# Another scheme of 20 products, with the first tap of a convolution moved to ScalarE and the sums of y to GpSimd

## Chip, cores, metric

One core of one Trainium2 chip. The metric is device time in microseconds of the whole program. Before: 2664.77 us, median of 3 runs (2663.69 to 2666.85).

## The reference, cut to what matters

```python
# x: (8, 4096, 192); 7-tap causal convolution, one softmaxed filter per head (8 heads of 24 channels)
out = np.einsum('hk,bskhg->bshg', w, x_unf)        # 32768 tokens of 192
h = x @ w_in                                       # 192 -> 2048
g = h * np.clip(h + 3.0, 0.0, 6.0) / 6.0
return g @ w_out                                   # 2048 -> 192
```

## The kernel before

Tokens are done in 32 blocks of 1024; the first is done directly, the other 31 in two stages each. In the **h stage**, 88 half matmuls with a fast scheme give h; ScalarE makes the relu and VectorE the gate, and g stays in SBUF as eight "places" (0 to 7), each 128 x 4 x 512 (four "units"). While it runs, GpSimd already makes some sums of places, unit by unit (`EARLY`), into extra places (8 and up). In the **product stage**, g @ w_out is made of 20 products of such places (or sums of them) with prepared sums of weights, two products side by side in one step, ten steps. VectorE makes large sums of places, GpSimd's queue issues DMA copies that add (`'sum', 'dma'`). A node is a partial result in one half of a PSUM bank. A copy (ScalarE) takes a node out of PSUM, a seed (ScalarE) puts such a copy into a node's half bank so that products are added to it, and a join (VectorE) adds a node and a copy. The convolution of the next block (seven taps on VectorE), the swap of y's halves by DMA and four sums of y run beside it. Each engine takes its instructions in the order of the program.

```python
EARLY = [(8, 3, 7, '+'), (3, 2, 3, '+'), (9, 2, 8, '+'), (10, 1, 0, '+'), (10, 10, 8, '-')]
STEPS = [
    ('conv',), ('mm', (6, 9, 56, 0, 1), (0, 0, 7, 1, 1)), ('conv',),
    ('mm', (4, 6, 56, 0, 0), (2, 3, 7, 1, 0)), ('sum', 6, 6, 9, '+'),
    ('mm', (9, 13, 49, 0, 1), (5, 8, 32, 1, 1)), ('sum', 2, 5, 6, '-'), ('copy', 7, (0, 0)),
    # ... cut: six more steps
    ('mm', (0, 1, 4, 0, 0), (1, 19, 2, 1, 0)),  # ... cut: joins and three outputs
]
# 'mm': two of (place, form of weights, node, half of a PSUM bank, opens the node)
# 'sum', to, a, b, sign: VectorE adds two places; 'sum', 'dma', to, from: a DMA adds
# 'copy', node, half tile | 'seed', node, ... | 'join', node, to, from, other, sign
# 'conv': next tap of the next block | 'ysums': the four sums of y

def tap(part, k, t):
    c = c_sb[:, k : k + 1]
    to = y[:, part, t : t + W]
    if k == 0:
        nc.vector.tensor_scalar(out=to, in0=x[:, part, t : t + W], scalar1=c, scalar2=None, op0=ALU.mult)
    else:
        nc.vector.scalar_tensor_tensor(out=to, in0=x[:, part, k + t : k + t + W], scalar=c, in1=to,
                                       op0=ALU.mult, op1=ALU.add)

def open(self, node, k):     # a node takes one half of a bank; two nodes can share a bank
    b = next((b for b, u in self.used.items() if k not in u), None)
    if b is None:
        b = take()
    # ... cut
```

## Time and profile before

| | before |
|---|---|
| median, us | 2664.77 |
| busy share of TensorE, VectorE, ScalarE, GpSimd | 92%, 82%, 49%, 43% |
| mean granted TensorE clock | 0.984 |
| product stage, h stage (means of the 30 blocks that another follows), us | 44.8, 38.0 |

The means by stage in this document are worked out from the trace's timeline of TensorE: from the first matmul with product weights to the first with h weights, and on to the next block.

### The profile page before, as it was taken

What the parts mean: (1) busy time and instruction counts of PE and PEld (TensorE: products, weight loads), DVE (VectorE), ACT (ScalarE), POOL (GpSimd) and SP (SyncE); (2) the same over time, 40 slices, a digit from 0 to 9 for tenths busy, and PEclk for the clock granted to TensorE, in tenths of its full rate; (3) what the DMA queues carried; (4) which work ended last, traced back from release to release, by engine and by line L of the source; (5) the groups of instructions that cost most, each with busy time, mean ns of one, the idle gap of its engine ahead of it and who ended that gap; (6) DMA issues with size and microseconds to landing.
All of it is one profiled execution on the core that took longest, in us unless ns stands there. A gap on an engine that the chain in (4) does not pass through costs nothing.

```text
span 2669.4 us, 40470 instructions
## 1 busy us (share of the span) xinstructions
PE 2458.6 (92%) x15976; PEld 981.8 (37%) x15976; DVE 2194.1 (82%) x2558; ACT 1312.1 (49%) x2233; POOL 1158.3 (43%) x856
## 2 busy tenths in 40 slices
PE   9988999999999999999899889999999998899888
PEld 5433343333333333433333333343333433333333
DVE  8688887888888888888888788888888878888786
ACT  7344555445554454544455444555445554455544
POOL 2634543445433455333553335543345433454334
PEclk9999999999999999999999999999999999999999
DMA  5143324433244432344323443324433244332443
GB/s 131 37 84 64 57 47 83 84 67 64 42 78 84 79 64 39 69 84 83 60 49 59 84 83 60 53 55 83 84 65 63 41 83 83 66 63 39 84 72 60
DMA packets 277934, 182.20 MB, mean 68 GB/s; under 512 B 208432, under 2 KB 213552, under 8 KB 277744
## 3 DMA queue, kind: packets, MB, share of 16 engines
q0 software_dynamic: 50688, 97.79, 21.8%
q1 hardware_dynamic: 226904, 81.69, 15.6%
q8 instruction: 125, 2.05, 0.3%
q14 instruction: 65, 0.53, 0.1%
q10 hardware_dynamic: 152, 0.13, 0.0%
HBM read 31.72 MB, written 25.17 MB: 21 GB/s over the span
## 4 chain that ended last, share of the span: by engine, by line
PE 64%; DVE 20%; issue 7%; DMA 5%; ACT 3%; SPq 0%; DVEq 0%; ACTq 0%
PE psum L338 46%; PE psum L621 16%; DVE g L568 5%; DMA y<-y 5%; DVE y L294 3%; DVE extra L568 3%; DVE parts L574 3%; DVE y L315 2%; DVE y L290 2%; PE psum L465 2%; DVE g L348 1%; ACT parts L639 1%; ACT r L344 1%; ACT psum L645 1%; SPq L307 0%
## 5 line engine op out<-in xcount | busy, mean ns | idle before, releaser
L621 PE MATMUL psum<-g,w_t 128*32 128x512 f32 x7440 | 1156.3, 607 | 119.1 <-ACT psum L645 66.4
L338 PE MATMUL psum<-y,w_in 64*128 64x512 f32 x3664 | 884.5, 591 | 0.0
L568 POOL TENSOR_TENSOR extra<-g 128x512 f32<-128x512 f32 x248 | 361.8, 1459 | 970.0 <-DVE g L348 970.0
L344 ACT ACTIVATE r<-psum,half 128x512 f32<-128x512 f32 x1024 | 642.0, 689 | 242.2 <-PE psum L338 232.5
L621 PE MATMUL psum<-extra,w_t 128*32 128x512 f32 x2480 | 578.3, 619 | 83.4 <-ACT psum L647 41.7
L348 DVE SCALAR_TENSOR_TENSOR g<-r,psum 128x512 f32<-128x512 f32 x1024 | 641.1, 680 | 5.4 <-ACT r L344 1.5
L338 PEld LDWEIGHTS psum<-y,w_in 64*128 64x128 f32 x3664 | 416.1, 187 | 397.4 <-issue 376.2
L621 PEld LDWEIGHTS psum<-g,w_t 128*32 128x32 f32 x7440 | 313.8, 112 | 623.3 <-issue 351.3
L338 PE MATMUL psum<-y,w_in_t 64*128 64x512 f32 x1984 | 523.5, 591 | 0.0
L639 ACT COPY parts<-psum 64x512 f32<-64x512 f32 x310 | 179.8, 580 | 692.8 <-PE psum L621 451.6
L430 DVE TENSOR_TENSOR psum<-psum,p 128x512 f32<-128x512 f32 x496 | 328.0, 696 | 224.2 <-PE psum L338 210.4
L294 DVE SCALAR_TENSOR_TENSOR y<-x,c_sb,y 128x1536 f32<-128x1536 f32 (+1 forms) x206 | 373.4, 1819 | 5.4
L338 PEld LDWEIGHTS psum<-y,w_in_t 64*128 64x128 f32 x1984 | 242.8, 186 | 200.9 <-issue 145.8
L621 PEld LDWEIGHTS psum<-extra,w_t 128*32 128x32 f32 x2480 | 143.6, 114 | 420.6 <-issue 263.0
L568 POOL TENSOR_TENSOR g<-g 128x512 f32<-128x512 f32 x124 | 158.1, 1275 | 289.6 <-DVE g L348 287.2
L574 DVE TENSOR_TENSOR parts<-parts 64x512 f32<-64x512 f32 x155 | 106.6, 688 | 156.3 <-ACT parts L639 152.2
L568 POOL TENSOR_TENSOR extra<-extra 128x512 f32<-128x512 f32 x124 | 218.4, 1762 | 9.7
L645 ACT COPY psum<-parts 64x512 f32<-64x512 f32 x279 | 163.2, 585 | 117.6 <-PE psum L621 110.8
L423 ACT COPY psum<-psum 128x512 f32<-128x512 f32 x248 | 138.9, 571 | 148.2 <-PE psum L338 133.5
L631 POOL DMA_DIRECT2D g<-g x124 | 152.2, 1950 | 86.0 <-DVE g L568 65.1
L568 DVE TENSOR_TENSOR g<-g 128x2048 f32<-128x2048 f32 x62 | 169.8, 2739 | 4.2
L568 POOL TENSOR_TENSOR extra<-g,extra 128x512 f32<-128x512 f32 x124 | 158.5, 1278 | 0.0
(60 smaller groups left out, 1019.5 us busy)
## 6 DMA issues: line engine op xcount, KB each, us to landing
g<-g POOLq DMA_DIRECT2D x124, 512.0 KB, 8.8
g<-extra POOLq DMA_DIRECT2D x62, 512.0 KB, 11.3
out_dram<-xt SPq DMA_DIRECT2D x384, 64.0 KB, 2.0
y<-y SPq DMA_DIRECT2D x62, 384.0 KB, 5.6
x<-in_x_dram SPq DMA_DIRECT2D x55, 388.5 KB, 5.6
stage<-in_moe_w_in_dram SPq DMA_DIRECT2D x16, 192.0 KB, 4.3
stage<-in_moe_w_out_dram SPq DMA_DIRECT2D x8, 384.0 KB, 5.0
x<-in_x_dram SPq DMA_DIRECT2D x7, 384.0 KB
```

What stands on the lines that cost most here:

```text
L294: nc.vector.scalar_tensor_tensor(out=to, in0=x[:, part, k + t : k + t + W], scalar=c, in1=to, op0=ALU.mult, op1=ALU.add,)
L338: nc.tensor.matmul(out=psum[:, b], lhsT=w[r], rhs=y[r, third_of_y], start=start, stop=stop, skip_group_check=onto,)
L344: nc.scalar.activation(r6, h, ACT.Relu, bias=half[:], scale=1.0 / 6.0)
L348: nc.vector.scalar_tensor_tensor(out=out, in0=r6, scalar=1.0, in1=h, op0=ALU.min, op1=ALU.mult)
L423: nc.scalar.copy(out=psum[:, bank["b"]], in_=psum[:, bank["a"]])
L430: nc.vector.tensor_tensor(out=psum[:, to], in0=psum[:, bank["b"]], in1=self.p5[:], op=ALU.add)
L568: engine.tensor_tensor(out=g_place(to)[:, u], in0=g_place(a)[:, u], in1=g_place(b)[:, u], op={"+": ALU.add, "-": ALU.subtract}[op],)
L574: nc.vector.tensor_tensor(out=out, in0=x, in1=y, op=op)
L621: nc.tensor.matmul(out=psum[col : col + QS, nodes.at[node][0]], lhsT=w[:, u, e * QS : (e + 1) * QS], rhs=g_place(place)[:, u], start=bool( ...
L631: nc.gpsimd.dma_start(out=g_place(args[1])[:, us], in_=g_place(args[2])[:, us], accum_op=ALU.add,)
L639: nc.scalar.copy(out=tile_half(*at), in_=nodes(node))
L645: nc.scalar.copy(out=nodes(node), in_=tile_half(*at))
```

## The change

Its intent: another scheme of 20 products, ordered anew, should make TensorE wait less for sums, seeds and joins; a fourth extra place makes room for sums that come earlier. VectorE gives its first tap to ScalarE and its sums of y to GpSimd. All else that the diff touches serves that: other sums of weights, a fifth tile for parts, two output buffers in place of four.

```diff
     EARLY = [
-        (8, 3, 7, '+'), (3, 2, 3, '+'), (9, 2, 8, '+'), (10, 1, 0, '+'), (10, 10, 8, '-'),
+        (8, 2, 3, '+'), (9, 1, 0, '-'), (9, 9, 3, '+'), ('dma', 3, 7), (10, 8, 7, '+'),
+        (11, 6, 10, '+'),
     ]
     STEPS = [
# (all steps replaced; the new ones:)
+        ('conv0',), ('conv',), ('mm', (4, 7, 56, 0, 1), (0, 0, 7, 1, 1)), ('conv',),
+        ('mm', (4, 6, 32, 0, 1), (2, 3, 7, 1, 0)), ('conv',),
+        ('mm', (5, 8, 32, 0, 0), (9, 4, 45, 1, 1)), ('conv',), ('copy', 7, (0, 0)),
+        ('seed', 49, 0, (0, 0), 1), ('seed', 54, 1, (0, 0), 1), ('sum', 'dma', 4, 6),
+        ('mm', (10, 13, 49, 0, 0), (11, 15, 48, 1, 1)), ('sum', 5, 5, 11, '+'),
+        ('copy', 45, (0, 0)), ('seed', 4, 0, (0, 0), 1), ('sum', 2, 5, 8, '-'),
+        ('seed', 41, 1, (0, 0), 1), ('mm', (0, 1, 4, 0, 0), (8, 5, 54, 1, 0)),
+        ('copy', 48, (0, 0)), ('sum', 6, 9, 2, '+'), ('seed', 1, 1, (0, 0), 1),
+        ('join', 49, (0, 1), None, (0, 0), 1), ('sum', 'dma', 9, 7),
+        ('mm', (6, 17, 42, 0, 1), (5, 18, 50, 1, 1)), ('conv',), ('seed', 9, 1, (0, 1), 1),
+        ('copy', 54, (0, 0)), ('conv',), ('mm', (4, 9, 56, 0, 0), (7, 10, 9, 1, 0)),
+        ('sum', 4, 4, 6, '-'), ('copy', 42, (1, 0)), ('seed', 18, 1, (1, 0), 1),
+        ('join', 50, (1, 1), None, (0, 0), 1), ('mm', (4, 14, 40, 0, 1), (2, 16, 18, 1, 0)),
+        ('sum', 5, 1, 5, '+'), ('ysums',), ('join', 32, (2, 0), None, (1, 1), -1),
# ... cut: two more steps, joins, three outputs; among them
+        ('out', 4, (16, 4)), ('copy', 41, (0, 0)), ('join', 32, (2, 0), (2, 0), (0, 0), -1),
+        ('join', 9, (1, 0), None, (0, 0), 1), ('two', 8, (2, 1), (1, 0), (1, 1), -1),
+        ('out', 2, (32, 8)), ('copy', 2, (0, 0)), ('join', 1, (0, 1), None, (1, 0), -1),
@@ the first tap
-            if k == 0:
+            if k == 0 and first is nc.scalar:
+                nc.scalar.mul(to, x[:, part, t : t + W], c)
+            elif k == 0:
@@ the sums of y
             elif op == "ysums" and more:
-                y_sums()
+                y_sums(nc.gpsimd)
@@ the places for sums
-        extra = ss.tile([P, 3, UNITS, N], F32, name="extra")
-        parts_ = cs.tile([P, 4, N], F32, name="parts")
+        extra = ss.tile([P, 4, UNITS, N], F32, name="extra")
+        parts_ = cs.tile([P, 5, N], F32, name="parts")
# ... cut: sums of weights, forms, output buffers, order at the start
```

## The prediction

> **What bounds the kernel now.** I read the page's busy shares first, then a table by stage, then what TensorE waits for, then the queues of VectorE and GpSimd at the start of one product stage. A block of 1024 tokens has two stages: the h stage (88 half matmuls and their gates) and the product stage (10 steps of two products each, steps 1 to 10 below). There are 31 such blocks. The table by stage, one block (span, then busy us and instructions of PE, PEld, DVE, ACT, POOL, then PE clock):
>
> ```profile
> 1211.90:1256.50 44.60, 38.26 (x322) 10.85 (x320) 37.98 (x30) 13.48 (x24) 18.08 (x12) 0.96 0.52 92
> 1256.50:1294.50 38.00, 38.00 (x180) 19.27 (x176) 30.65 (x51) 27.13 (x46) 17.68 (x15) 1.00 0.21 39
> ```
>
> The h stage is TensorE without a gap; its 38.0 us can't shrink by this change. The product stage takes 44.6 us, though one unhindered step is a row of 32 records in 3.64 us with its tail, 3.44 us when the next follows (64 records in 7.07): ten steps are 34.4 + 0.2 = 34.6 us. So 10.0 us a block are lost there, 310 us in all; that is the whole prize. Who causes it, from the waits of TensorE:
>
> ```profile
> PE psum L621 <- DVE parts L574: 94.2, 60, 3.4
> PE psum L621 <- ACT psum L645: 66.6, 63, 1.4
> PE psum L621 <- ACT psum L647: 41.7, 31, 1.3
> ```
>
> These make 202 us, 6.5 us a block; the rest is slow matmuls at half clock after the gaps, and ends of steps. The releasers are joins and seeds: VectorE and ScalarE come late. Why, the timeline at the stage's start shows, VectorE first, then GpSimd (start, us, what):
>
> ```profile
> 1213.94 1.81 DVE L290 TENSOR_SCALAR y<-x,c_sb 128x1536 f32<-128x1536 f32 x1
> 1215.78 2.62 DVE L294 SCALAR_TENSOR_TENSOR y<-x,c_sb,y 128x1536 f32<-128x1536 f32 x1
> 1218.33 3.37 DVE L568 TENSOR_TENSOR g<-g,extra 128x2048 f32<-128x2048 f32 x1
> 1221.80 3.19 DVE L568 TENSOR_TENSOR g<-g 128x2048 f32<-128x2048 f32 x1
> 1224.90 1.81 DVE L294 SCALAR_TENSOR_TENSOR y<-x,c_sb,y 128x1536 f32<-128x1536 f32 x1
> 1226.63 2.28 DVE L568 TENSOR_TENSOR extra<-g,extra 128x2048 f32<-128x2048 f32 x1
> ```
> ```profile
> 1215.50 1.29 POOL L568 TENSOR_TENSOR extra<-g,extra 128x512 f32<-128x512 f32 x1
> 1216.74 2.81 POOL L568 TENSOR_TENSOR extra<-g 128x512 f32<-128x512 f32 x1
> 1219.62 3.21 POOL L568 TENSOR_TENSOR extra<-extra 128x512 f32<-128x512 f32 x1
> ```
>
> The two engines take turns. A tap alone is 1.81 us, beside GpSimd 2.62; a sum alone 2.28, beside it 3.37 or 3.19; GpSimd's 1.29 becomes 2.81 and 3.21. The ends fit strict alternation: GpSimd ends at 1216.79, the tap at 1218.40, GpSimd at 1219.55, the sum at 1221.70, GpSimd at 1222.83, the next sum at 1224.99. Net holds: tap 1.66, GpSimd's sum 1.14, large sum 2.15. The one-source first tap (1.81) beside GpSimd is not slowed. So VectorE runs without a pause from the stage's start until step 5, which waits for it.
>
> **What the Trainium skill says.** (1) GPSIMD Engine Reference, section 1, Specifications: GpSimd shares its SBUF interfaces with VectorE and contends with VectorE instructions that have two SBUF inputs. The trace agrees: 1.81 against 2.62. (2) VectorE: DVE Perf Modes, the section on the TRN2 errata: a two-source fp32 addition takes (N+151)/0.96 ns; for N = 2048 that is 2291, the trace has 2.28 us. (3) TensorE: Matmul & The Clock Gate, Part 1: after an idle window of about 3.4 us the array falls to half clock, until about 3.4 us of work. Here it fell even in stages with shorter gaps (PE clock 0.96 above), so a longer gap will hardly escape.
>
> **The change part by part.** Times count from the start of a product stage; waits are those of the changed program as built, in its order on each engine. The number of products, matmuls, transposes and stores is the same.
>
> *First tap to ScalarE.* VectorE loses 1.81 us. On ScalarE a 128x128 scaling took 390 ns and a 128x512 one 721, so 0.86 ns an element; 1536 elements are estimated at 1.6 us. ScalarE's last relu ends at 1.35 (1213.28 - 1211.93), so the product is there at 2.95; VectorE, free at 2.1, starts its second tap then. Gain on the path 0.9 us, not 1.8.
>
> *Early sums and four taps in front.* The last unit's gate ends at 2.1. GpSimd then owes 5 sums and one DMA issue, VectorE four taps, all with two SBUF inputs, so they alternate: sum 8 until 3.4; then tap 1.66, sum 1.14, tap, sum (place 9 at 9.0), tap (10.6; the DMA issue of 1.2 beside it), sum (place 10 at 11.8), tap (13.4), sum: place 11 at 3.4 + 4 x 1.66 + 4 x 1.14 = 14.6. Step 3 needs 9 at about 9.5: no wait. Step 4 starts at 10.3 and needs the last quarter of 11 at 12.9: it waits 1.7 and ends at 15.6. Step 5 runs to 19.0.
>
> *The chain to step 6.* VectorE: 5 += 11 starts at 14.6 (it needs 11), 16.9; 2 = 5 - 8, 19.2; then 6 = 9 + 2, then the join of node 49, 0.7, which shares a bank with step 6's node, so step 6 waits for it. But 6 = 9 + 2 overwrites what the DMA sum 4 += 6 reads, and this DMA is queued on GpSimd behind sum 11: two issues from 14.6 to 17.0. A DMA sum of 512 KB landed after 5.2 us at the least and 10.2 in the middle; at the measured 187 GB/s each takes 2.8 us of transfer. The second lands between 21 and 23, say 22. So the sum ends at 24.3, the join at 25.0, step 6 starts at 25.1 where step 5 ended at 19.0: **6 us of gap**. Without the DMA it would be 22.3, still over 3 us.
>
> *Steps 6 to 10.* Step 6 to 28.5, 7 to 32.0. The sum 4 = 4 - 6 overwrites step 7's operand and feeds step 8: TensorE waits 2.3. Step 8 34.3 to 37.8; step 9, whose bank waits for a join, 38.0 to 41.4; a seed in the other half of step 9's bank takes 0.7; step 10 to 45.6. Sum of the waits: 1.7 + 6.0 + 2.3 + 0.2 + 0.7 = 10.9, with 34.6 of work 45.5. To this comes half clock after the 6 us gap: a window of 3.4 us costs 1.7 of work when it falls on running steps; I take 1.5. **Product stage: 47 us**, was 44.6.
>
> *Sums of y to GpSimd.* VectorE loses 2.62 us and the wait for the swap of y (0.87), which were in front of step 10's joins. That is what the change gains. The swap starts at about 28.6 (two taps after the join) and takes 6.8 as in the chain before (1242.86 to 1249.67); GpSimd's four sums of 1.27, some delayed by joins, end near 43, before the h stage needs them. Free, but what held step 10 is then no longer VectorE's total but the chain above. VectorE also gets 14 joins in place of 11 (3 x 0.69).
>
> *The end of the stage.* Only the last output is put off, so after step 10 ScalarE copies (0.6), VectorE does two joins (1.4), then ScalarE frees a bank, which the fifth matmul of the h stage needs: there at 2.8 after the start, where TensorE wants it at 1.7; with the two copies behind it the h stage loses about 1.4 us: 39.4.
>
> *Start.* One more weight sum and three more negations, about 2 us once, mostly beside matmuls.
>
> Sum: 47.0 + 39.4 = 86.4 against 82.6, 3.8 x 31 = 118, and 2: 2665 + 120 = **2785 us**.
>
> **The rivals.** A: *the relief wins*. VectorE loses 4.4 us a block and steps wait less: were the DMA sum to land by 19 and the clock to stay, the stage is 34.6 + 1.7 + 3.3 + 3.2 = 42.8 and the block 82.2 with the late h start, 81 without: 2615 to 2650. For it speaks that seeds and joins caused all waits before and that now most seeds come a step earlier; against it, that three whole sums in a row stand between place 11 and step 6. B: *the chain of sums as above but no clock loss and an early DMA (21)*: stage 44.6, block 84: 2710. C: *the DMA is slower*, 10 us or more as its median says, and half clock lasts two windows: stage 49 to 50, block 89: 2860. D: if GpSimd did not alternate with VectorE but came first, place 11 is there at about 10, the DMA lands at 18 and the stage is near 42: as A. The measured alternation speaks against it.
>
> **Range and chances.** Between B and C lies most of it: 2700 to 2850. Faster by 2% needs under 80.9 us a block, which even A barely reaches: 0.06. Within 2% is 80.9 to 84.3, A's worse half and B: 0.14. Slower: 0.80.
>
> **What would show it.** In the profile after: the largest wait of TensorE is on the join (same line, VectorE) before step 6, 5 to 7 us, 31 times; one on the sum of VectorE before step 8, 2.3 us; one on GpSimd's sum in step 4, 1 to 2 us; PE clock under 1.0 in most product stages; 39 to 40 us for the h stage; the swap's wait on VectorE gone; the first tap on ScalarE near 1.6 us. Wrong if the product stage is under 43 us: then the DMA sum lands earlier or the two engines do not take turns as I read it. If the h stage alone grows, my count of late joins was right and the chain wrong.

## The result, and the profile after

2864.07 us, median of 4 runs (2862.03 to 2867.15), beside 2665.23 us of before: ratio 1.0747, 95% interval 1.0728 to 1.0766. It is slower, as predicted, but by 199 us where 120 were predicted, and outside the range. (Ratios here are the mean time of one kernel's runs over that of the other's of the same rounds, so not quite the ratio of the medians quoted.)

The same table by stage for one block of the changed kernel (span, then busy us and instructions of PE, PEld, DVE, ACT, POOL, then PE clock, DMA share and GB/s):

```profile
1202.98:1251.80 48.82, 38.41 (x322) 12.25 (x320) 36.85 (x26) 10.25 (x17) 26.15 (x16) 0.93 0.39 71
1251.80:1291.30 39.50, 38.72 (x178) 19.45 (x176) 31.91 (x51) 27.86 (x48) 17.86 (x15) 1.00 0.31 55
```

The product stage grew from 44.6 to 48.8 us and the h stage from 38.0 to 39.5. The product stage has a clock of 0.93 where it had 0.96. Over the 30 blocks that another follows the means are 49.3 (was 44.8) and 39.5 (was 38.0). What TensorE waits for (us in total, times, longest):

```profile
PE psum L639 <- DVE parts L592: 201.4, 37, 8.2
PE psum L639 <- DVE g L581: 77.0, 31, 2.5
PE psum L345 <- DVE parts L592: 23.5, 30, 0.8
PE psum L639 <- POOL extra L581: 23.1, 30, 0.8
PE psum L639 <- ACT psum L659: 21.3, 31, 0.7
```

The waits for seeds of ScalarE, 108 us before, are down to 21; but one join now costs 201 us. The timeline of TensorE in that block shows where, with the idle time before a row in brackets:

```profile
1217.70 0.62 PE L639 MATMUL psum<-extra,w_t 128*32 128x512 f32 x2 [0.80 <-POOL extra L581]
...
1228.64 9.04 PE L639 MATMUL psum<-g,w_t 128*32 128x512 f32 x64 [6.45 <-DVE parts L592]
...
1240.16 4.05 PE L639 MATMUL psum<-g,w_t 128*32 128x512 f32 x34 [2.48 <-DVE g L581]
...
1248.14 3.74 PE L639 MATMUL psum<-g,w_t 128*32 128x512 f32 x32 [0.68 <-ACT psum L659]
```

Counted from the stage's start at 1202.98, these are step 4's wait for place 11 (at 14.7), the gap before step 6 (starts at 25.7), the wait before step 8 and that before step 10. Steps 6 and 7 are the row of 64 records: 9.04 us, where 64 records took 7.07 before. That is the half clock. VectorE and then GpSimd in the same stage:

```profile
1205.84 10.69 DVE L301 SCALAR_TENSOR_TENSOR y<-x,c_sb,y 128x1536 f32<-128x1536 f32 x4 [0.76 <-ACT y L295]
1217.68 4.62 DVE L581 TENSOR_TENSOR g<-g,extra 128x2048 f32<-128x2048 f32 x2 [1.16 <-POOL extra L581]
1225.57 2.29 DVE L581 TENSOR_TENSOR g<-extra,g 128x2048 f32<-128x2048 f32 x1 [3.27 <-DMA g<-g]
1227.90 0.68 DVE L592 TENSOR_TENSOR parts<-psum,parts 64x512 f32<-64x512 f32 x1
```
```profile
1214.98 2.67 POOL L581 TENSOR_TENSOR extra<-g,extra 128x512 f32<-128x512 f32 x1
1217.60 2.43 POOL L587 DMA_DIRECT2D g<-g  x2
```

GpSimd's first row is the sum to place 11. The four taps take 10.69 us where four alone take 7.2: they alternate with GpSimd. GpSimd's last sum ends at 1217.65, VectorE's two large sums start on it, then VectorE waits 3.27 us for the DMA that GpSimd could issue only then, makes 6 = 9 + 2, and the join lets TensorE go on.

The last block tells the same without taps, since no block follows whose convolution is to be made. VectorE, then TensorE, in the last product stage (it starts at 2803.63):

```profile
2814.23 4.62 DVE L581 TENSOR_TENSOR g<-g,extra 128x2048 f32<-128x2048 f32 x2 [8.49 <-POOL extra L581]
2821.88 2.29 DVE L581 TENSOR_TENSOR g<-extra,g 128x2048 f32<-128x2048 f32 x1 [3.03 <-DMA g<-g]
```
```profile
2824.94 9.60 PE L639 MATMUL psum<-g,w_t 128*32 128x512 f32 x64 [3.93 <-DVE parts L592]
```

Without taps in its way GpSimd is done at 10.4 in place of 14.7, and still VectorE waits 3 us for the DMA, and steps 6 and 7 still take 9.60 us, as at half clock. From the start of this stage to the end of the program it is 56.6 us, before 46.1.

### The profile page after: what moved, and what is told of

It is laid out like the page before. It is cut to its first block, busy times and chain, and to the rows that moved or that the text cites.

```text
span 2860.2 us, 40589 instructions
## 1 busy us (share of the span) xinstructions
PE 2502.0 (87%) x15976; PEld 1017.9 (36%) x15976; DVE 2196.5 (77%) x2501; ACT 1234.5 (43%) x2080; POOL 1408.3 (49%) x977
## 3 DMA queue, kind: packets, MB, share of 16 engines
q1 hardware_dynamic: 226904, 81.69, 14.4%
q8 instruction: 125, 2.05, 0.3%
## 5 line engine op out<-in xcount | busy, mean ns | idle before, releaser
L639 PE MATMUL psum<-g,w_t 128*32 128x512 f32 x7440 | 1055.3, 630 | 298.2 <-DVE parts L592 199.9
L639 PE MATMUL psum<-extra,w_t 128*32 128x512 f32 x2480 | 468.1, 594 | 24.9 <-POOL extra L581 23.1
L301 DVE SCALAR_TENSOR_TENSOR y<-x,c_sb,y 128x1536 f32<-128x1536 f32 (+1 forms) x206 | 447.8, 2180 | 28.1 <-ACT y L295 22.7
L581 POOL TENSOR_TENSOR extra<-extra,g 128x512 f32<-128x512 f32 x248 | 385.3, 1565 | 9.7
L653 ACT COPY parts<-psum 64x512 f32<-64x512 f32 x217 | 126.0, 581 | 592.7 <-PE psum L639 545.9
L322 POOL TENSOR_TENSOR y<-y 128x512 f32<-128x512 f32 x120 | 219.8, 1849 | 290.9 <-DMA y<-y 288.5
L587 POOL DMA_DIRECT2D extra<-g x62 | 75.5, 1449 | 263.2 <-DVE g L581 252.4
L581 POOL TENSOR_TENSOR extra<-g,extra 128x512 f32<-128x512 f32 x124 | 200.1, 1614 | 9.7
L592 DVE TENSOR_TENSOR parts<-psum,parts 64x512 f32<-64x512 f32 x279 | 190.1, 687 | 13.1 <-PE psum L639 5.7
L592 DVE TENSOR_TENSOR parts<-parts 64x512 f32<-64x512 f32 x155 | 137.6, 888 | 63.8 <-ACT parts L653 59.8
```

The lines of the kernel that those rows point to most:

```text
L322: engine.tensor_tensor(out=y[:, o], in0=y[:, a], in1=y[:, b], op=op)
L581: engine.tensor_tensor(out=g_place(to)[:, u], in0=g_place(a)[:, u], in1=g_place(b)[:, u], op={"+": ALU.add, "-": ALU.subtract}[op],)
L587: nc.gpsimd.dma_start(out=g_place(to)[:, u], in_=g_place(a)[:, u], accum_op=ALU.add)
L592: nc.vector.tensor_tensor(out=out, in0=x, in1=y, op=op)
L639: nc.tensor.matmul(out=psum[col : col + QS, nodes.at[node][0]], lhsT=w[:, u, e * QS : (e + 1) * QS], rhs=g_place(place)[:, u], start=bool( ...
L653: nc.scalar.copy(out=tile_half(*at), in_=nodes(node))
```

## The experiments

Fourteen kernels were run, in four rounds of chip time, each on another chip; all gave correct results, also those with extra matmuls. Each was timed in three rounds beside the kernel before (4 timed runs each, 7 of before, whose medians were 2667 to 2671). Differences told below are of medians; between rounds the ratios make them up to some 8 us different. "Step 6 starts at" and the like are means over the inner blocks whose waits came in the usual pattern, 20 at the least (b_moves, whose scheme differs, and the stage means count all). Half clock is the sum of the stretches in which the trace's record of granted clock stands at 0.5 (with a last stretch of 3 to 11 us that begins near the end of each run): 87 us in the kernel before, 234 us in the changed one.

| kernel | median us | ratio to before | product stage | h stage | step 6 starts at | half clock |
|---|---|---|---|---|---|---|
| before | 2665 | 1 | 44.8 | 38.0 | | 87 |
| changed | 2864.07 | 1.0747 | 49.3 | 39.5 | 25.7 | 234 |
| a_warm | 2828.93 | 1.0596 | 48.4 | 39.5 | 26.1 | 77 |
| a_warm2 | 2802.59 | 1.0492 | 47.5 | 39.5 | 26.0 | 20 |
| a_place11 | 2752.96 | 1.0318 | 46.1 | 39.5 | 22.5 | 141 |
| a_sum8 | 2788.66 | 1.0448 | 47.0 | 39.5 | 25.7 | 245 |
| a_copy41 | 2858.25 | 1.0699 | 49.9 | 38.8 | 25.8 | 264 |
| a_tap_back | 2857.35 | 1.0697 | 49.1 | 39.6 | 24.3 | 309 |
| a_tap_back_warm2 | 2755.59 | 1.0310 | 45.8 | 39.6 | 24.6 | 11 |
| a_ysums_back | 2930.46 | 1.0969 | 51.7 | 39.5 | 25.8 | 305 |
| b_moves | 2629.32 | 0.9851 | 42.7 | 38.7 | | 72 |
| c_sums | 2648.84 | 0.9916 | 43.2 | 38.8 | 22.5 | 113 |
| c_front2 | 2637.98 | 0.9876 | 43.0 | 38.8 | 21.1 | 191 |
| c_front3 | 2631.38 | 0.9856 | 42.4 | 38.9 | 21.1 | 161 |
| c_front2_warm | 2622.46 | 0.9818 | 42.3 | 38.8 | 21.1 | 7 |
| c_front3_warm | 2570.34 | 0.9619 | 40.4 | 38.9 | 21.1 | 7 |

**Is it the clock that was mis-sized? a_warm and a_warm2.** Extra matmuls whose result nobody reads fill the gaps, so that TensorE is busy there without anything else being moved.

```diff
+            elif op == "warm":
+                for n in range(args[0]):
+                    col = n % 4 * QS
+                    nc.tensor.matmul(
+                        out=psum[col : col + QS, free_banks[-1]], lhsT=w_t[:, 0, 0, 0:QS],
+                        rhs=g_place(7)[:, 0], start=True, stop=True,
+                        tile_position=(0, col), skip_group_check=True,
+                    )
-        ('mm', (0, 1, 4, 0, 0), (8, 5, 54, 1, 0)),
+        ('mm', (0, 1, 4, 0, 0), (8, 5, 54, 1, 0)), ('warm', 24),
# a_warm2 also, in front of step 8:
-        ('mm', (4, 9, 56, 0, 0), (7, 10, 9, 1, 0)),
+        ('mm', (4, 9, 56, 0, 0), (7, 10, 9, 1, 0)), ('warm', 10),
```

> The changed kernel with 24 extra matmuls (5.2 us at full clock) between steps 5 and 6, into a bank that nobody reads; they wait for nothing new, and lie inside the 6.5 us gap. Theory (half clock is the mis-sized term): TensorE has no idle window any more, the clock stays at 1.0 in the product stage, steps 6 and 7 take 6.9 to 7.1 us in place of 8.9, steps 8 and 9 7.2 in place of 7.8; step 6 still starts 25.7 us into the stage; product stage 46.7 in place of 49.3, whole kernel 2780 to 2790. Rival (steps 6 to 9 are slow because DMA sums, taps and joins take memory from the matmuls, or because the chip lowers the clock under load): steps 6 and 7 stay at 8.5 to 9 us, the kernel at 2855 to 2870 or more.

Steps 6 and 7 fell from 8.9 to 7.2 us, as the clock theory had it and its rival had not. But the kernel came to 2829, not 2780 to 2790: step 6 started 0.4 us later, and steps 8 and 9 rose from 7.8 to 8.2 us. Half clock had moved to the next gap, the 2.48 us before step 8. So that was filled too:

> As a_warm (24 extra matmuls in the gap before step 6), and 10 more (2.15 us) in the 2.48 us gap before step 8. In a_warm steps 6 and 7 fell from 8.9 to 7.2 us as expected, but half clock came 3.4 us a block later, in steps 8 and 9 (8.2 us), where the theory had none. Theory now: the clock falls after any 3.4 us window that is mostly idle, a gap of 2.5 us is enough; with both gaps filled half clock is under 20 us in all, steps 6 and 7 take 7.1, steps 8 and 9 7.3, product stage 47.2 to 47.7, kernel 2790 to 2805. Rival (steps 8 and 9 are slowed by the joins, the sums of y and the swap that run beside them): steps 8 and 9 stay above 8 us and the kernel at 2820 or more.

2802.59 us and half clock of 20 us in all, as expected. Two lines of the timeline of TensorE for a_warm2 (idle time before a row in brackets):

```profile
1293.46 7.07 PE L639 MATMUL psum<-g,w_t 128*32 128x512 f32 x64 [1.29 <-DVE parts L592]
...
1310.99 3.74 PE L639 MATMUL psum<-g,w_t 128*32 128x512 f32 x32 [0.68 <-ACT psum L667]
```

Steps 6 and 7 are back at 7.07. Nothing of the chain was taken away, and the kernel is 61 us faster with 34 matmuls more in each product stage. So half clock cost about 2 us a block on balance (61 / 31), about 2.3 without the 0.3 us by which step 6 came later. In the blocks with a late step 6 the DMA sum landed late, up to 23.9 us into the stage in place of 22.4; why it did is open.

**Is the gap before step 6 made by the DMA sum? a_place11.** The sum 9 + 2 goes to a place that the DMA does not read.

```diff
-('sum', 6, 9, 2, '+')            +('sum', 11, 9, 2, '+')
-('mm', (6, 17, 42, 0, 1), ...)   +('mm', (11, 17, 42, 0, 1), ...)
-('sum', 4, 4, 6, '-')            +('sum', 4, 4, 11, '-')
```

> The changed kernel with the sum 9 + 2 written to place 11 (free by then) in place of place 6, so that it doesn't wait for the DMA sum 4 += 6 to have read place 6. Theory (the DMA sum gates the gap before step 6): VectorE's wait for the DMA (103.8 us in all) is gone, step 6 starts at 22.3 us in place of 25.7, gap 3.2 in place of 6.5; each block 3.4 us shorter, and up to 2.6 more if the clock then holds: 2680 to 2760. Rival (the gap is VectorE's own work or the late place 11 alone): step 6 moves by under 1 us, 2835 to 2865.

Step 6 starts at 22.47 with a gap of 3.28, to a tenth as expected. In the block that starts at 1250.63, VectorE and then TensorE:

```profile
1265.32 4.62 DVE L581 TENSOR_TENSOR g<-g,extra 128x2048 f32<-128x2048 f32 x2 [1.16 <-POOL extra L581]
1270.04 2.29 DVE L581 TENSOR_TENSOR extra<-extra,g 128x2048 f32<-128x2048 f32 x1
```
```profile
1273.10 1.07 PE L639 MATMUL psum<-extra,w_t 128*32 128x512 f32 x2 [3.28 <-DVE parts L592]
```

The wait for the DMA before the third sum is gone. The DMA sum held step 6 for 3.3 us; the chain of three sums and a join behind place 11 holds it for the rest.

**The wait before step 8. a_sum8.**

```diff
-('sum', 4, 4, 6, '-')            +('sum', 8, 4, 6, '-')
-('mm', (4, 14, 40, 0, 1), ...)   +('mm', (8, 14, 40, 0, 1), ...)
```

> The changed kernel with the sum 4 - 6 written to place 8 (free after step 5) and step 8 reading it there, so that it doesn't wait for step 7 to have read place 4. Theory: VectorE's wait for TensorE before this sum (167.5 us in all) and TensorE's 2.48 us before step 8 go away, nothing else moves: 2.4 us a block, 2785 to 2795. Rival (another wait takes its place, a join or the sums of y): 2840 or more, with a wait of 1 us or more before step 9 or 10 that was not there.

2788.66: 75 us, 2.4 a block, and no other wait came. The prediction's 2.3 us for this was a true cost.

**The late h stage. a_copy41.**

```diff
-('copy', 41, (0, 0)), ('join', 32, (2, 0), (2, 0), (0, 0), -1), ('join', 9, (1, 0), None, (0, 0), 1)
+('copy', 41, (3, 0)), ('join', 32, (2, 0), (2, 0), (3, 0), -1), ('join', 9, (1, 0), None, (3, 0), 1)
```

> The changed kernel with node 41 copied to another half tile, so that the copy of node 2, which frees the bank of the fifth matmul of the h stage, needn't wait for two joins. Theory (the late end of the stage costs the h stage 1.4 to 1.5 us through this bank): h stage 38.4 to 38.7 in place of 39.5, kernel 2825 to 2840. Rival (the h stage is long because VectorE comes late with its joins and additions): h stage within 0.3 us of 39.5, 2855 or more.

The h stage fell to 38.82, near the expectation, and TensorE's wait of 0.8 us in it is gone, so the bank did hold it. But that is half of the story: of the 1.5 us by which the h stage had grown 0.8 are still there (in the one block looked at, as short delays in its first 16 us), and their cause is open. And the kernel gained only 6 us: the product stage rose by 0.6 us, with 30 us more of half clock. That the one explains the other is likely, not shown for this kernel alone.

**The parts that moved between engines. a_tap_back, a_ysums_back.** Each puts one of them back on VectorE.

```diff
# a_tap_back
-conv = conv_units(i + 1, [slice(0, K3)], first=nc.scalar) if i + 1 < NB else []
+conv = conv_units(i + 1, [slice(0, K3)]) if i + 1 < NB else []
# a_ysums_back
-                y_sums(nc.gpsimd)
+                y_sums()
```

> The changed kernel with the first tap back on VectorE. Theory (the alternation with GpSimd and the DMA sum behind it gate the stage, not VectorE's load): VectorE's one-source first tap lets GpSimd do two sums beside it, place 11 comes at 13.0 us in place of 14.7, the DMA sum lands some 1.5 us earlier, step 6 starts at 24.2 in place of 25.7: 1 to 2 us a block LESS although VectorE does 1.8 us more, 2805 to 2840. Rival (VectorE's load is what counts): 0.9 to 1.8 us a block more, 2890 to 2920.

> The changed kernel with the sums of y back on VectorE. Theory (this part of the change is a gain, hidden by the rest): the four sums, 2.6 us, stand before the join that step 9's bank waits for and before the joins of step 10, which moves step 9 by 1.5 to 2.6 us: 2905 to 2945. Rival (GpSimd's sums of y cost as much by contending with the joins, 1.34 us for a join of 0.68): within 10 us of 2864.

The sums of y on GpSimd are a gain in the changed kernel: 66 us by the medians (2930.46 without), 59 by the ratios. How much of it is theirs alone is not shown, since half clock is 71 us longer without them. With the first tap back, step 6 started at 24.3, as expected: more work for VectorE, an earlier step 6. The start of that stage, VectorE and then GpSimd:

```profile
1291.79 1.81 DVE L297 TENSOR_SCALAR y<-x,c_sb 128x1536 f32<-128x1536 f32 x1
1293.64 10.91 DVE L301 SCALAR_TENSOR_TENSOR y<-x,c_sb,y 128x1536 f32<-128x1536 f32 x4
```
```profile
1292.06 2.52 POOL L581 TENSOR_TENSOR extra<-g 128x512 f32<-128x512 f32 x2
```

GpSimd makes two sums in 2.52 us while VectorE makes the one-source tap; in the changed kernel it made one and then had to let a two-source tap pass. But the kernel gained only 7 us, against the expected 24 to 59. Half clock had risen to 309 us. The same kernel with the gaps filled as in a_warm2 was to tell whether that was all:

```diff
# against a_tap_back: the two steps of a_warm2
-        ('mm', (0, 1, 4, 0, 0), (8, 5, 54, 1, 0)),
+        ('mm', (0, 1, 4, 0, 0), (8, 5, 54, 1, 0)), ('warm', 24),
-        ('mm', (4, 9, 56, 0, 0), (7, 10, 9, 1, 0)),
+        ('mm', (4, 9, 56, 0, 0), (7, 10, 9, 1, 0)), ('warm', 10),
```

> The changed kernel with the first tap back on VectorE and with the extra matmuls of a_warm2 in both gaps. In a_tap_back step 6 started at 24.3 us as expected (25.7 before), but the kernel gained only 7 us; half clock had risen to 309 us in all. Theory (the earlier step 6 is real and half clock ate it): with the clock held, 1.3 to 1.7 us a block less than a_warm2, 2750 to 2765, half clock under 20 us. Rival (the first tap on VectorE costs later in the stage what it gives before step 6): level with a_warm2, 2795 to 2810.

2755.59, against 2802.59 of a_warm2: 47 us, 1.5 a block. The earlier step 6 was real, and half clock had eaten it. The move of the first tap to ScalarE, meant as a relief, costs in this scheme.

**The two engine moves on the old scheme. b_moves.** The kernel before with both moves and nothing else.

```diff
# against the kernel before
-            if k == 0:
+            if k == 0 and first is nc.scalar:
+                nc.scalar.mul(to, x[:, part, t : t + W], c)
+            elif k == 0:
-                y_sums()
+                y_sums(nc.gpsimd)
-conv = conv_units(i + 1, [slice(0, K3)]) if i + 1 < NB else []
+conv = conv_units(i + 1, [slice(0, K3)], first=nc.scalar) if i + 1 < NB else []
```

> The kernel before with its own scheme of products and only the two engine moves of the change: first tap on ScalarE, sums of y on GpSimd. Theory (the moves relieve VectorE, the new scheme loses): the waits of steps 5 and 10 shrink, 2 to 3.5 us a block less, 2560 to 2610, faster than before. Rival (the moves cost as much as they give, because GpSimd's sums of y then contend with VectorE's joins and the h stage waits for them): within 1% of before or slower.

2629.32, ratio 0.9851 (0.9822 to 0.9880): a gain clear of noise, though under 2% and short of the expected 55 us at least. The first join's step and the three behind it start within 0.15 us of where they did in the kernel before (its first wait ends at 15.34 us in both): the first tap gave nothing here either. VectorE came to its first large sum earlier and waited for GpSimd instead; in the block that starts at 1276.76:

```profile
1283.19 3.35 DVE L570 TENSOR_TENSOR g<-g,extra 128x2048 f32<-128x2048 f32 x1 [1.17 <-POOL extra L570]
```

The join is made 17.03 us into the stage, as in the kernel before. The gain is the wait before step 10: that step starts 1.8 us earlier. By their place in the order it is the sums of y that stood there; no run moves them alone on this scheme. The h stage lost 0.7 us of it (38.7). TensorE's longest waits:

```profile
PE psum L623 <- ACT psum L647: 66.1, 62, 1.4
PE psum L623 <- ACT psum L649: 41.6, 31, 1.3
PE psum L623 <- DVE parts L576: 41.2, 30, 1.4
```

Joins cost 41 us in place of 94; the other two rows are as before. So the two moves together are a gain on the old scheme, and the new scheme with its order is what lost.

**Do the repairs add up, and can the new scheme win? c_sums and c_front2, c_front3.** c_sums joins a_place11, a_sum8 and a_copy41. In c_front2 and c_front3 two or three taps, not four, stand in front of step 3, and the rest behind the join:

```diff
# c_front3 against c_sums
-        ('mm', (5, 8, 32, 0, 0), (9, 4, 45, 1, 1)), ('conv',), ('copy', 7, (0, 0)),
+        ('mm', (5, 8, 32, 0, 0), (9, 4, 45, 1, 1)), ('copy', 7, (0, 0)),
-        ('copy', 54, (0, 0)), ('conv',), ('mm', (4, 9, 56, 0, 0), (7, 10, 9, 1, 0)),
-        ('sum', 8, 4, 11, '-'), ('copy', 42, (1, 0)), # ... cut
+        ('copy', 54, (0, 0)), ('conv',), ('sum', 8, 4, 11, '-'), ('conv',), ('mm', (4, 9, 56, 0, 0), (7, 10, 9, 1, 0)),
+        ('copy', 42, (1, 0)), # ... cut
# c_front2: one ('conv',) less in front of step 3, one more at the end of this
```

> The three repairs of single waits together: sum 9 + 2 to place 11 (no wait for the DMA sum), sum 4 - that to place 8 (no wait for step 7), node 41 copied elsewhere (h stage). Theory (the waits are independent, each worth what it measured alone): product stage 46.1 - 2.4 = 43.6, h stage 38.8, kernel 2630 to 2680, level with the kernel before. Rival (the waits hide each other, and the clock falls for the gap of 3.3 us all the same): 2690 or more.

2648.84: 215 us less than the changed kernel, where the three alone gained 111, 75 and 6, 192 in all. None of the waits hides another.

> c_sums with two taps in front of step 3 in place of four, the other four behind the join before step 6, and the sum to place 8 between them. Theory (GpSimd's late sums are late because they alternate with the four taps): place 11 at 11.5 to 12 us in place of 14.7, step 4 doesn't wait, step 6 starts at 19.5 to 20 with a gap of about 2 us, the swap of y lands at 36 and its sums are ready for the h stage; product stage 38 to 39, block 76.5 to 78.5, kernel 2480 to 2550. Rival (VectorE's load of 68.7 us a block, or late sums of y, is then the bound): waits of 1 us and more on sums of y in the h stage, block 80 or more, 2590 or more.

> As c_front2, with three taps in front and three behind. Theory: place 11 at 13.0, step 6 at 20.7 with a gap of 2.3, swap 1.8 us earlier than with two: product stage 39 to 40, 2510 to 2580; between c_sums and c_front2. Rival (late sums of y bound c_front2): faster than c_front2.

Both missed by far. Place 11 came at 13.3 in c_front2, not at 11.5 to 12: I had left out the DMA issue (1.2 us) that stands in GpSimd's queue between its sums. So two taps gave no earlier step 6 than three (21.1 both). And steps 6 to 9 took 17.0 to 17.6 us in place of 14.2, with half clock of 161 and 191 us: a gap of 3.28 us is enough for it.

At last the gap before step 6 of both was filled:

```diff
-        ('mm', (0, 1, 4, 0, 0), (8, 5, 54, 1, 0)),
+        ('mm', (0, 1, 4, 0, 0), (8, 5, 54, 1, 0)), ('warm', 8),     # c_front2_warm
+        ('mm', (0, 1, 4, 0, 0), (8, 5, 54, 1, 0)), ('warm', 12),    # c_front3_warm
```

> c_front2 with 8 extra matmuls (1.7 us) in the gap left before step 6. Theory (a gap of 2 us can still bring half clock in some blocks): half clock, in all blocks together, 60 to 100 us in c_front2 and under 20 here, 15 to 40 us less than c_front2. Rival (a gap of 2 us is harmless): within 10 us of c_front2.

> c_front3 with 12 extra matmuls (2.6 us) in the gap of 3.28 us before step 6. In c_front2 and c_front3 half clock was 191 and 161 us, and steps 6 to 9 took 17.0 to 17.6 us in place of 14.2. Theory (in c_front3 nothing but the clock stands between step 6 and the end of the stage): half clock under 20 us, step 10 at 36.0 to 36.7, product stage 39.7 to 40.5, kernel 2545 to 2575, the fastest of all. Rival (a late join before step 9 as in c_front2_warm takes over): a wait of 1 us or more before step 9, 2600 or more.

With the gap filled, c_front2 gained only 16 us: in step 9 TensorE waited 1.8 us for a late join (the taps stand in front of it). c_front3 has no such wait, gained 61 us and is the fastest of all: **2570.34 us, ratio 0.9619 (0.9589 to 0.9648)** to the kernel before. TensorE's longest waits in it:

```profile
PE psum L639 <- ACT psum L667: 21.2, 31, 0.7
PE psum L639 <- DVE parts L592: 21.1, 30, 0.7
```

So the new scheme is not slower as such: with another order, its sums in free places and the gap filled it is faster. That it would also beat the old scheme treated alike is not shown: the gaps of b_moves, with 72 us of half clock, were not filled.

## Why the prediction was right or wrong

The direction was right (0.80 on slower), and so was the mechanism in the main; sizes were wrong, the loss to half clock most of all, and with them the time and the range. Point by point:

- *Early sums alternate with the taps, place 11 at 14.6.* Right: 14.7. Step 4's wait, 1.7 predicted, was 0.8; step 5 then ends at 19.2, where 19.0 was predicted. (By the lines shown a tap's net hold is 1218.40 - 1216.79 = 1.61, not 1.66, which makes 14.4.)
- *The DMA sum and three sums in a row hold step 6, gap 6 us.* Right: gap 6.5, start 25.7 in place of 25.1. (The landing time of 10.2 us in the middle, which the prediction gives for the kernel before, is 10.5 in its trace.) a_place11 took the DMA's part away and hit the predicted 22.3 (22.47).
- *Step 8 waits 2.3, step 10 0.7.* Right: 2.48 and 0.68.
- *The sums of y are a gain that the chain hides.* Right in sign: some 60 us by a_ysums_back, part of which may be half clock.
- *The h stage 39.4.* The number is right: 39.5. The reason is half of it: a_copy41 took the bank's wait away and 38.8 was left, not 38.0. So the fit to a tenth is luck.
- *The first tap gains 0.9 us on the path.* Wrong. It starts VectorE's two-source taps earlier, and these hold GpSimd; with the clock held, undoing it gains 1.5 us a block. The chain's sum was right only because its end, 14.6, was walked through with both engines. The reading that VectorE's load sets the waits of the kernel before has the same fault: its step 5 waits first for a seed of ScalarE (1.39 us) and then for the join, and in b_moves the two rows of waits for seeds, 108 us, stayed.
- **The step that failed: "a window of 3.4 us costs 1.7 of work when it falls on running steps; I take 1.5."** The record of the clock shows half clock for 6.8 us, two windows, in nearly every block. Steps 6 and 7 took 1.95 us more than the 6.9 that I had planned at full clock, steps 8 and 9 0.7 more than 7.1: 2.65. At full clock, in most blocks of a_warm2, these steps take 7.07 and 7.3. So half clock cost about 2.3 us in place of 1.5, as a_warm2 says too, and the remaining 0.35 is that I had planned the steps themselves too short.
- *The last block counted as any other.* It lost 10.4 us, not 3.8: without taps the kernel before loses most of its waits (the rest of the program from that stage's start, 46.1 us), the changed one keeps the DMA and the clock.

The sum, from the two profiled runs: 2860.2 - 2669.4 = 190.8, where 120 were predicted. The 30 full periods are 88.87 us in place of 82.85, so 6.02 longer, not 3.8: 67 us too little. These 2.2 us each are 1.15 of steps 6 to 9 (0.8 of clock, 0.35 of steps planned too short), 0.64 of the later step 6, 0.44 of steps 8 and 10, 0.11 by which I had rounded the stage down and 0.13 of the h stage, less 0.25 because the mean block before was 82.85 and not 82.6. The last block is 6.6, and the 2 us at the start did not come. So half clock, the term furthest off, explains 0.8 of the 2.2 us; the other 1.4 are smaller shortfalls of the chain, nearly all on the same side, the late step 6 first (the DMA sum landed at 22.4, not 22). a_warm2 says the same: with almost no half clock it still takes 2803 us, 65 more than the 2738 that the prediction gives without its clock term (2785 - 31 x 1.5).

Of the rivals, A was wrong; D came true only in the last block, where no taps stand in the way (place 11 at 10.4, the DMA's wait ended at 18.3); C had the clock right, two windows, and the DMA wrong (the second DMA sum landed 7.1 us after its issue, not 10); that its 2860 is close to 2864 is luck.

The range was too narrow on that side because I treated the clock as a small addition to a known chain, and the chain as known to a tenth. It is a loss of its own, which moved to another gap when one was closed (a_warm) and grew when another wait was taken away (a_tap_back). It made the expectations of a_warm, a_tap_back and c_front3 miss, and probably that of a_copy41. c_front2 missed its range even with the gap filled (2622, where 2550 was the upper end), and b_moves missed for other reasons: the first tap gave nothing and the h stage lost 0.7 us.

Which windows fall to half clock can be read from the kept traces, though no run was made for it. In each trace the stretches of half clock inside the blocks start on one grid of 3.41 us. I counted the idle time of TensorE in every window of this grid, in the fourteen traces that have such stretches. At full clock, all 375 windows with more than 2.05 us idle were followed by half clock, and none of the 8890 with less than 1.85; between the two it went both ways. Half clock ended after every window with under 0.73 us idle and after none with over 0.78. It need not be one gap: in b_moves two gaps of 1.4 us, of which 1.87 to 2.36 us fell into one window, were enough. So what counts is the idle time in a window, and where the grid falls on the gaps; the latter I can't foretell for a new kernel, nor was this count tried as a forecast.

## What to carry to other kernels

Before work is moved from a busy engine to another, ask what the freed engine starts earlier and whom that holds: here two-source work of VectorE and sums of GpSimd take turns, so an earlier tap made a later sum, and a DMA queued behind that sum held the matmuls. Look for values overwritten in place while a slow reader still needs them; writing a sum to a free place was worth 75 and 111 us. And when TensorE's waits come to 2 us or more within 3.4 us in every round, first see what keeping it busy gives, before judging any other repair: with half clock in play, true gains of 1.5 us a block did not show.

## What the Trainium skill lacked or had wrong

- TensorE: Matmul & The Clock Gate, Part 1 and the table "Why this matters for your kernels", which advises no idle gaps above about 3 us. Here a gap of 2.48 us was enough (a_warm: 77 us of half clock, nearly all behind that gap; 20 us when it was filled too), and in b_moves two gaps of 1.4 us were. The stretches of half clock inside the blocks last 3.41 us or two or three times that and start on a grid of 3.41 us, which agrees with the page's window. How much idle time makes a window count as idle is not told there; here it was about 1.9 to 2.0 us of 3.41. The page tells of such losses from shorter pauses too, but as a remedy names other loops and, for measuring, matmuls in front. That matmuls without use, placed in the gaps of a running kernel, are one, worth 61 us in a_warm2 and again in c_front3_warm, is not told there.
- GPSIMD Engine Reference, section 1, Specifications: it names the contention with two-input VectorE instructions and gives no times for it. (That whole instructions are held is told elsewhere in the skill and is no lack.) Here GpSimd's sum of 1.29 us took 2.67 beside a tap, four taps took 10.69 us in place of 7.2, and a one-source tap of 1.81 us was not touched.
- DMA: Bandwidth & Descriptors, Anatomy of one DMA — SWDGE (gpsimd) path: its fit, 2.0 us and the bytes over 436e3, gives 3.2 us for 512 KB. The adding DMA copies from SBUF to SBUF landed after 5.1 us in the middle and 5.0 at the least (changed kernel, into g), and moved 187 GB/s when several were under way (kernel before). That page has no figure for copies that add.
